# A retention layer with a two-layer network behind it: the first two groups ordered by a list scheduler, loads in one software queue, transposes moved to DMA

## The chip, the core and the metric

The kernel runs on one NeuronCore of a Trainium2 chip. Its engines take their instructions in program order, each from its own stream: TensorE (PE, with its weight loads as PEld), VectorE (DVE), ScalarE (ACT), GpSimd (POOL) and SyncE (SP). DMAs are issued from SP's stream (the hardware queue q1) or from POOL's (the software queue q0), and are moved by 16 DMA engines that all queues share. The metric is the device time of one execution in microseconds; lower is better. A profiled execution gives a span, from the first to the last instruction.

## What is computed

For 4 sequences and 8 heads of width 64, over 768 steps, a state is decayed and updated, and read by q; then two matrices with `h * cos(h)` between them act on all 3,072 tokens.

```python
for t in range(S):                       # gamma = 1 - 2**(-5 - head)
    state = gamma * state + einsum('bhd,bhe->bhde', k[:, :, t], v[:, :, t])
    y[:, :, t] = scale * einsum('bhd,bhde->bhe', q[:, :, t], state)
x = y.transpose(0, 2, 1, 3).reshape(3072, 512)
h = x @ w_in                             # 512 x 2048
out = (h * cos(h)) @ w_out               # 2048 x 512
```

## The kernel before, in words

**Tiling.** Time is cut into chunks of 128 steps, six to a sequence. Two sequences go together, so there are 12 *pairs* p (two sequences b, one chunk c = p mod 6), and two pairs make a *group* g of 512 tokens, six in all. Within a chunk the recurrence is a masked product of q and k; what came before enters through the state.

**Steps of a pair.** *Load*: q, k, v of each of the two sequences, 128 steps on the partitions, 256 KB each, in float32 (`load`, L103). *Convert* to bf16, with the decay multiplied into q and v (`conv_q` L146, `conv_v` L151, `conv_k` L156). *T* (`stage_t`, L163): 16 TensorE transposes of q and k by an identity, into PSUM, and two copies to `qkt`. *A* (`stage_a`, L182): 16 products of k and q, row-tiled, two at a time, into four PSUM banks. *Masks* (`stage_m`, L197): four on VectorE. *Y* (`stage_y`, L205): the masked A times v plus q times the old state, column-tiled, copied by ScalarE into `xt`, which is x transposed. *S* (L227): k times v added up in the bank `st_ps`, copied into `stb` for the next pair.

**Steps of a group.** *F*: for each of 16 row blocks f of w_in four matmuls of 128 x 512 into a bank (`unit_f`, L250), cosine on ScalarE (the Sin table with half pi added, L244), the product on VectorE into `gt` (L248). A half unit (`pair_f`, L258) does two f for the 256 tokens of one pair, with eight matmuls of 128 x 256. *O* (`unit_o`, L274): for each 128 tokens j sixteen matmuls of 128 x 512 with w_out, in four parts, then a copy by ScalarE and a 256 KB store from SP.

**What sets the order.** It is written out by hand; each engine's stream follows the order of the program text. Semaphore waits come from the tiles that are read and written. PSUM has seven rotating banks (`Banks`, taken and given in the order of the text) beside `st_ps`; converted tiles have three buffers, float32 loads five, `cosb` three, `ob` four. L289 to L304 issue the first loads: SP's queue gets all q and the first v of most pairs, POOL's queue k, the other v, and both weight matrices (float32 in memory, bf16 in the core), with POOL's own conversions between. L310 to L355 interleave pairs 0 to 3 with half units of groups 0 and 1. From L359 on a loop over g does, in each of 16 slots s, one F unit of group g (not for g = 1, whose F is done already) and one part of O of group g-1; eight slots go to each pair p = 2(g+1) and p+1: T at r = 1, A at 2, conversions of pair p+1 at 4, Y and S at 6, loads of pair p+3 after that.

Of the kernel before, what the change touches and what calls it, by code (L numbers as in the profile page):

```python
# [10 lines left out]
FP32 = mybir.dt.float32  # L11
# [5 lines left out]
class Banks:  # L17
# [8 lines left out]
    def give(self, t):  # L26
        self.free_list.append(t)


@with_exitstack  # L30
def kernel(
# [11 lines left out]
    C = 128  # L43
# [8 lines left out]
    PRE = 5  # L52

# [4 lines left out]

# [10 lines left out]

# [8 lines left out]


    qf = [[sb([128, H, D], FP32, f"qf{i}_{b}") for b in range(2)] for i in range(PRE)]  # L80
    kf = [[sb([128, H, D], FP32, f"kf{i}_{b}") for b in range(2)] for i in range(PRE)]
    vf = [[sb([128, H, D], FP32, f"vf{i}_{b}") for b in range(2)] for i in range(PRE)]
    ob = [sb([128, DM], FP32, f"ob{i}") for i in range(4)]
    NB = 3
# [15 lines left out]

    SRC = {"q": (qf, q), "k": (kf, k), "v": (vf, v)}

    def load(eng, p, names):  # L103
        bp, c = divmod(p, NC)
        for n in names:
            t, src = SRC[n[0]]
            b = int(n[1])
            eng.dma_start(
                out=t[p % PRE][b],
                in_=src[2 * bp + b, :, ds(c * C, C)].rearrange("h t d -> t h d"))  # L110

    def load_w_in(r):
        nc.gpsimd.dma_start(
            out=w_in_sb[:, :, ts(r, 512)],
            in_=moe_w_in[:, ts(r, 512)].rearrange("(i p) f -> p i f", p=128))
# [5 lines left out]


    nc.gpsimd.iota(pos, pattern=[[C, NC]], base=1, channel_multiplier=1,
                   allow_small_or_imprecise_dtypes=True)
    load(nc.sync, 0, ("q0", "q1", "v0"))
    load(nc.sync, 1, ("q0", "q1"))
    load(nc.gpsimd, 0, ("k0", "k1", "v1"))
    make_identity(nc, ident)
    nc.vector.memset(lnsc, math.log(scale))
    nc.vector.memset(halfpi, math.pi / 2.0)  # L130
    nc.vector.memset(mask, 1.0)
# [4 lines left out]
    nc.scalar.activation(out=gk, in_=lgp, func=AF.Exp, scale=-1.0)  # L136
    nc.gpsimd.affine_select(out=mask, in_=mask, compare_op=ALU.is_ge, fill=0.0,
# [5 lines left out]
    def bc(g, c):  # L143
        return g[:, c, :].unsqueeze(2).to_broadcast([128, H, D])

    def conv_q(p, eng):  # L146
        for b in range(2):
            eng.tensor_tensor(out=qs[p % NB][:, b], in0=qf[p % PRE][b],
                              in1=bc(gq, p % NC), op=ALU.mult)

    def conv_v(p, eng):  # L151
        for b in range(2):
            eng.tensor_tensor(out=vs[p % NB][:, b], in0=vf[p % PRE][b],
                              in1=bc(gk, p % NC), op=ALU.mult)

    def conv_k(p, on_act):  # L156
        for b in range(2):
            if on_act:
                nc.scalar.copy(out=ks[p % NB][:, b], in_=kf[p % PRE][b])
            else:  # L160
                nc.vector.tensor_copy(out=ks[p % NB][:, b], in_=kf[p % PRE][b])

    def stage_t(p, split):  # L163
        n = p % NB
        for b in range(2):
            bank = banks.take()
            tr = bank.bitcast(BF16).rearrange("p (w a t) -> p w a t", w=2, a=HP)
            for w, src in enumerate((qs[n], ks[n])):
                for a in range(HP):
                    nc.tensor.transpose(tr[:, w, a, :], src[:, b, 2 * a : 2 * a + 2, :], ident)  # L170
            if split and b == 1:
                nc.vector.tensor_copy(out=qkt[n][:, b], in_=tr)
            else:
                nc.scalar.copy(out=qkt[n][:, b], in_=tr)
            banks.give(bank)

    def qt(n, b, a):
        return qkt[n][:, b, 0, a, :]

    def kt(n, b, a):  # L180
        return qkt[n][:, b, 1, a, :]
    def stage_a(p):  # L182
        n = p % NB
        todo = []
        for b in range(2):
            bk = [banks.take(), banks.take()]
            ap = [t.rearrange("p (a t) -> p a t", a=HP) for t in bk]
            for a in range(HP):
                for j in range(2):
                    po = 64 * j  # L190
                    nc.tensor.matmul(ap[j][:, a, :], lhsT=kt(n, b, a)[po : po + 64, :],
                                     rhs=qt(n, b, a)[po : po + 64, :],
                                     tile_position=(po, 0))
            todo.append((b, bk, ap))
        return todo

    def stage_m(p, item):  # L197
        b, bk, ap = item
        for j in range(2):
            nc.vector.tensor_tensor(  # L200
                out=am[p % 2][b][j], in0=ap[j],
                in1=mask.unsqueeze(1).to_broadcast([128, HP, 128]), op=ALU.mult)
            banks.give(bk[j])

    def stage_y(p, copy_st=nc.vector.tensor_copy):  # L205
        c = p % NC
        n = p % NB
        for b in range(2):
            bank = banks.take()
            yp = bank.rearrange("p (a t) -> p a t", a=HP)  # L210
            for a in range(HP):
                if c > 0:
                    for j in range(2):
                        nc.tensor.matmul(  # L214
                            yp[ts(j, 64), a, :], lhsT=stb[p % 2][:, b, a, ts(j, 64)],
                            rhs=qt(n, b, a), start=True, stop=False,
                            skip_group_check=True)
                for j in range(2):
                    nc.tensor.matmul(
                        yp[ts(j, 64), a, :], lhsT=vs[n][:, b, 2 * a + j, :],  # L220
                        rhs=am[p % 2][b][j][:, a, :], start=(c == 0), stop=True,
                        skip_group_check=True)
            nc.scalar.copy(out=xt[(p // 2) % 2][:, :, ts(2 * (p % 2) + b, C)], in_=yp)
            banks.give(bank)
        if c == NC - 1:
            return
        for b in range(2):  # L227
            for a in range(HP):
                for j in range(2):
                    h = 2 * a + j  # L230
                    nc.tensor.matmul(  # L231
                        st_ps[ts(j, 64), b, a, :], lhsT=ks[n][:, b, h, :],
                        rhs=vs[n][:, b, h, :], start=(c == 0 and b == 0 and a == 0),
                        stop=True, skip_group_check=True)
        for j in range(2):
            copy_st(out=stb[(p + 1) % 2][ts(j, 64), :, :, ts(j, 64)], in_=st_ps[ts(j, 64)])  # L236


    f_no = [0]

    def act(bank, out):
        cb = cosb[f_no[0] % 3]
        f_no[0] += 1
        nc.scalar.activation(out=cb, in_=bank, func=AF.Sin, bias=halfpi)  # L244
        if len(out.shape) == 3:
            cb = cb.rearrange("p (f t) -> p f t", f=2)
            bank = bank.rearrange("p (f t) -> p f t", f=2)
        nc.vector.tensor_tensor(out=out, in0=bank, in1=cb, op=ALU.mult)  # L248

    def unit_f(g, f):  # L250
        bank = banks.take()
        for i in range(KIN):
            nc.tensor.matmul(bank, lhsT=w_in_sb[:, i, ts(f, 128)], rhs=xt[g % 2][:, i, :],  # L253
                             start=(i == 0), stop=(i == KIN - 1))
        act(bank, gt[g % 2][:, f, :])
        banks.give(bank)

    def pair_f(p, r):  # L258

        g, hf = divmod(p, 2)  # L260
        for f in (4 * r, 4 * r + 2):
            bank = banks.take()
            for e in range(2):
                for i in range(KIN):
                    nc.tensor.matmul(bank[:, ts(e, 256)], lhsT=w_in_sb[:, i, ts(f + e, 128)],  # L265
                                     rhs=xt[g % 2][:, i, ts(hf, 256)],
                                     start=(i == 0 and e == 0), stop=(i == KIN - 1),
                                     skip_group_check=True)
            act(bank, gt[g % 2][:, f : f + 2, ts(hf, 256)])
            banks.give(bank)  # L270

    o_bank = {}

    def unit_o(g, j, part):  # L274
        if part == 0:
            o_bank[0] = banks.take()
        bank = o_bank[0]
        for f in range(4 * part, 4 * part + 4):
            nc.tensor.matmul(bank, lhsT=gt[g % 2][:, f, ts(j, 128)], rhs=w_out_sb[:, f, :],  # L279
                             start=(f == 0), stop=(f == KOUT - 1))  # L280
        if part == 3:
            o = ob[j % 4]
            nc.scalar.copy(out=o, in_=bank)
            banks.give(bank)
            bp, c = divmod(2 * g + j // 2, NC)
            nc.sync.dma_start(out=out[ds((2 * bp + j % 2) * S + c * C, C), :], in_=o)


    load(nc.gpsimd, 1, ("k0", "k1", "v0", "v1"))  # L289
    load_w_in(0)  # L290
    load_w_in(1)
    for p in (2, 3):
        load(nc.sync, p, ("q0", "q1"))
# [8 lines left out]
    for r in range(4):  # L302
        load_w_out(r)
# [109 lines left out]
```

## Time and profile before

| | |
|---|---|
| runs of the kernel | 225.5 us median of 3 (224.25 to 225.9) |
| profiled execution | 223.9 us span; the page gives no other total for it |
| PE, DVE, ACT, POOL busy | 207.6, 124.4, 121.2, 83.4 us |
| granted TensorE clock | 1.000 |
| first matmul; first F of group 2; last matmul | 4.89; 78.67; 219.9 us |
| DMA | 29.65 MB written (27.26 MB read from memory): queue q1 37,776 packets for 14.95 MB, q0 7,344 for 14.42 MB |

The profile is read by stretches, since the share of busy time hides where it is lost: the 40 slices of the page show which engine is full when. The chain that ended last is followed back from the last instruction, and gives for each piece its start, its length and what it was. Columns of a stretch are its bounds, then per engine the busy time and the instructions, the granted clock, the DMA engines' share and GB/s written. A matmul of 512 columns is shown with 379 ns, but they overlap: four of them follow one another in 0.864 us.

### The profile page before, as it was taken

What the parts mean: (1) busy time and instruction counts of PE and PEld (TensorE: products, weight loads), DVE (VectorE), ACT (ScalarE), POOL (GpSimd) and SP (SyncE); (2) the same over time, 40 slices, a digit from 0 to 9 for tenths busy, and PEclk for the clock granted to TensorE, in tenths of its full rate; (3) what the DMA queues carried; (4) which work ended last, traced back from release to release, by engine and by line L of the source; (5) the groups of instructions that cost most, each with busy time, mean ns of one, the idle gap of its engine ahead of it and who ended that gap; (6) DMA issues with size and microseconds to landing.
All of it is one profiled execution on the core that took longest, in us unless ns stands there. A gap on an engine that the chain in (4) does not pass through costs nothing.

```text
span 223.9 us, 4434 instructions
## 1 busy us (share of the span) xinstructions
PE 207.6 (93%) x1792; PEld 118.7 (53%) x1792; DVE 124.4 (56%) x201; ACT 121.2 (54%) x180; POOL 83.4 (37%) x95
## 2 busy tenths in 40 slices
PE   1479899989999999999999999999999999999992
PEld 0357788958655554554554554554554544444440
DVE  4375969979583727638538528528527333443000
ACT  3475897766625255565565565565565545444121
POOL 7989848603999957190520610000000000000000
PEclk9999999999999999999999999999999999999999
DMA  6999999999949793925511511011011011110221
GB/s 159 333 233 274 220 282 199 197 298 259 276 97 314 216 268 76 256 81 171 129 47 59 132 47 53 0 50 47 0 50 47 0 50 47 47 47 0 97 78 63
DMA packets 45140, 29.65 MB, mean 132 GB/s; under 512 B 35456, under 2 KB 39552, under 8 KB 45120
## 3 DMA queue, kind: packets, MB, share of 16 engines
q1 hardware_dynamic: 37776, 14.95, 26.1%
q0 software_dynamic: 7344, 14.42, 25.4%
q8 instruction: 14, 0.23, 0.4%
q14 instruction: 6, 0.05, 0.1%
HBM read 27.26 MB, written 6.29 MB: 150 GB/s over the span
## 4 chain that ended last, share of the span: by engine, by line
PE 83%; DMA 4%; ACT 4%; DVE 4%; SPq 2%; issue 1%; DVEq 0%; ACTq 0%
PE bank_64 L279 15%; PE bank_63 L279 6%; PE bank_67 L253 5%; PE bank_69 L253 5%; PE bank_65 L253 5%; PE bank_66 L279 5%; DMA qf_1_81<-in_q_dram 4%; PE bank_68 L279 4%; PE bank_66 L253 4%; PE bank_68 L253 4%; PE bank_63 L253 4%; PE bank_65 L279 3%; PE bank_63 L265 2%; PE bank_69 L265 2%; PE bank_66 L265 2%; PE bank_68 L265 2%
## 5 line engine op out<-in xcount | busy, mean ns | idle before, releaser
L253 PEld LDWEIGHTS <-w_in_sb 128*128 128x128 bf16 x256 | 23.8, 98 | 26.9
L279 PEld LDWEIGHTS <-gt_137 128*128 128x128 bf16 x192 | 18.8, 98 | 22.7
L279 PEld LDWEIGHTS <-gt_136 128*128 128x128 bf16 x192 | 18.3, 98 | 21.4
L265 PEld LDWEIGHTS <-w_in_sb 128*128 128x128 bf16 x256 | 25.2, 100 | 5.1 <-issue 0.8
L279 PE MATMUL bank_64<-w_out_sb,gt_136 128*128 128x512 bf16 x96 | 24.2, 380 | 0.0
L279 PE MATMUL bank_64<-w_out_sb,gt_137 128*128 128x512 bf16 x64 | 16.4, 379 | 0.0
L279 PE MATMUL bank_63<-w_out_sb,gt_136 128*128 128x512 bf16 x48 | 12.3, 379 | 0.0
L279 PE MATMUL bank_66<-w_out_sb,gt_137 128*128 128x512 bf16 x48 | 11.8, 379 | 0.0
L236 DVE CAST stb_133<-st_ps 64x512 bf16<-64x512 f32 x10 | 6.9, 687 | 2.6 <-PE st_ps L231 2.4
L253 PE MATMUL bank_63<-xt_134,w_in_sb 128*128 128x512 bf16 x32 | 8.2, 380 | 0.0
L279 PE MATMUL bank_68<-w_out_sb,gt_137 128*128 128x512 bf16 x32 | 8.2, 379 | 0.0
L279 PE MATMUL bank_65<-w_out_sb,gt_136 128*128 128x512 bf16 x32 | 7.9, 380 | 0.0
L244 ACT ACTIVATE cosb_140<-bank_65,halfpi 128x512 bf16<-128x512 f32 x8 | 5.5, 689 | 4.3 <-PE bank_65 L253 3.3
L244 ACT ACTIVATE cosb_139<-bank_67,halfpi 128x512 bf16<-128x512 f32 x7 | 4.8, 687 | 5.3 <-PE bank_67 L253 4.3
L244 ACT ACTIVATE cosb_138<-bank_69,halfpi 128x512 bf16<-128x512 f32 x7 | 4.9, 693 | 4.6 <-PE bank_69 L253 4.3
L214 PEld LDWEIGHTS <-stb_133 128*64 128x64 bf16 x96 | 5.2, 109 | 3.8 <-issue 3.8
L253 PE MATMUL bank_68<-xt_135,w_in_sb 128*128 128x512 bf16 x28 | 7.2, 379 | 0.0
L244 ACT ACTIVATE cosb_138<-bank_63,halfpi 128x512 bf16<-128x512 f32 x7 | 4.8, 689 | 3.6 <-PE bank_63 L253 2.2
L244 ACT ACTIVATE cosb_140<-bank_67,halfpi 128x512 bf16<-128x512 f32 x6 | 4.1, 691 | 4.5 <-PE bank_67 L253 4.3
L244 ACT ACTIVATE cosb_138<-bank_66,halfpi 128x512 bf16<-128x512 f32 x6 | 4.1, 687 | 4.1 <-PE bank_66 L253 2.4
L253 PE MATMUL bank_65<-xt_134,w_in_sb 128*128 128x512 bf16 x24 | 6.2, 380 | 0.0
L253 PE MATMUL bank_67<-xt_134,w_in_sb 128*128 128x512 bf16 x24 | 6.2, 380 | 0.0
(398 smaller groups left out, 518.5 us busy)
## 6 DMA issues: line engine op xcount, KB each, us to landing
w_in_sb<-in_moe_w_in_dram POOLq DMA_DIRECT2D x4, 512.0 KB, 10.2
w_out_sb<-in_moe_w_out_dram POOLq DMA_DIRECT2D x4, 512.0 KB, 15.4
out_dram<-ob_108 SPq DMA_DIRECT2D x6, 256.0 KB, 2.1
out_dram<-ob_109 SPq DMA_DIRECT2D x6, 256.0 KB, 2.0
out_dram<-ob_110 SPq DMA_DIRECT2D x6, 256.0 KB, 2.1
out_dram<-ob_111 SPq DMA_DIRECT2D x6, 256.0 KB, 2.0
qf_0_78<-in_q_dram SPq DMA_DIRECT2D x3, 256.0 KB, 4.4
qf_1_79<-in_q_dram SPq DMA_DIRECT2D x3, 256.0 KB, 5.0
```

Source lines behind the costliest of these rows:

```text
L214: nc.tensor.matmul(yp[ts(j, 64), a, :], lhsT=stb[p % 2][:, b, a, ts(j, 64)], rhs=qt(n, b, a), start=True, stop=False, skip_group_check=True)
L236: copy_st(out=stb[(p + 1) % 2][ts(j, 64), :, :, ts(j, 64)], in_=st_ps[ts(j, 64)])
L244: nc.scalar.activation(out=cb, in_=bank, func=AF.Sin, bias=halfpi)
L253: nc.tensor.matmul(bank, lhsT=w_in_sb[:, i, ts(f, 128)], rhs=xt[g % 2][:, i, :], start=(i == 0), stop=(i == KIN - 1))
L265: nc.tensor.matmul(bank[:, ts(e, 256)], lhsT=w_in_sb[:, i, ts(f + e, 128)], rhs=xt[g % 2][:, i, ts(hf, 256)], start=(i == 0 and e == 0), s ...
L279: nc.tensor.matmul(bank, lhsT=gt[g % 2][:, f, ts(j, 128)], rhs=w_out_sb[:, f, :], start=(f == 0), stop=(f == KOUT - 1))
```

## The change

Pairs 0 to 5, A of pair 6, F of groups 0 and 1 and O of group 0 are no longer ordered by hand: while the program is built, a list scheduler (`Plan`) places each step on an engine, by ranks, its own costs, free banks and supposed landing times of loads, and emits the steps in the order of their starts. Group 0's first four f are half units, the other twelve whole units over both pairs; group 1 stays in half units. All loads but q of pair 0 go through POOL, both sequences in one DMA of 512 KB, in the order of `LOADS`; the scheduler puts VectorE, ScalarE or GpSimd on conversions and copies. Pairs 5 to 11 (the sixth pair on, `DMA_T`) have q and k transposed by two DMAs each from SP, between tiles in the core, in place of T. The loop starts at g = 2; loads of pair p+3, conversions and transposes of pair p+1 are issued at r = 0 of pair p, and after slot r = 3 one block does A of pair p+1, then Y and S of pair p, then the masks. The last O tile is done in two halves of 256 columns, stored from SP and ACT. The Sin table is loaded at the start, and the identity is made by a VectorE fill and one GpSimd step.

```diff
+class Plan:
...
+    def run(self, start, cold_until=0.0):
+        free = dict(start)
+        mode = [None]
+        left = list(self.ops)
+        t = 0.0
+        while left:
...
+                best = None
+                for op in left:
+                    if e not in op["engines"]:
+                        continue
+                    r = self.ready(op)
+                    if r is None:
+                        continue
+                    if r > t + 1e-9:
+                        nxt.append(r)
+                        continue
+                    ok = True
+                    for k, n in op["take"]:
+                        tk = sorted(self.tokens[k])
+                        n += op["spare"] if k == "bank" else 0
+                        if len(tk) < n:
+                            ok = False
+                        elif tk[n - 1] > t + 1e-9:
+                            nxt.append(tk[n - 1])
...
+                    key = (op["rank"] + (0.5 if op["mode"] and op["mode"] != mode[0] else 0), op["n"])
+                    if best is None or key < best[0]:
+                        best = (key, op)
+                if best is None:
+                    continue
+                op = best[1]
+                left.remove(op)
+                c = op["cost"][e] if isinstance(op["cost"], dict) else op["cost"]
+                busy, took = c if isinstance(c, tuple) else (c, c)
+                if e == "E":
...
+                        busy, took = busy + self.SWITCH, took + self.SWITCH
+                        mode[0] = op["mode"]
+                for k, n in op["take"]:
+                    self.tokens[k].sort()
+                    del self.tokens[k][:n]
+                op.update(eng=e, start=t, free=t + busy, done=t + took, lat=self.LAT[e])
+                free[e] = t + busy
+                if op["mb"]:
+                    self.dma = max(self.dma, t + busy + 1.6) + op["mb"] / op["rate"]
...
+    def emit(self):
+        for op in sorted(self.ops, key=lambda o: (o["start"], o["n"])):
+            op["fn"](op["eng"])
...
-    def load(eng, p, names):
-        bp, c = divmod(p, NC)
-        for n in names:
-            t, src = SRC[n[0]]
-            b = int(n[1])
-            eng.dma_start(
-                out=t[p % PRE][b],
-                in_=src[2 * bp + b, :, ds(c * C, C)].rearrange("h t d -> t h d"))
+    def load(eng, p, names):
+        bp, c = divmod(p, NC)
+        for n in names.split():
+            t, src = SRC[n[0]]
+            if len(n) == 1:
+                eng.dma_start(
+                    out=t[p % PRE].rearrange("p b h d -> p (b h) d"),
+                    in_=src[ds(2 * bp, 2), :, ds(c * C, C), :].rearrange(
+                        "b h t d -> t (b h) d"))
...
+    def dma_t(p, w):
+        n = p % NB
+        nc.sync.dma_start_transpose(
+            out=qkt[n][:, w].rearrange("p b a t -> p (b a) t"),
+            in_=(qs, ks)[w][n].rearrange("p b h d -> p (b h d)"))
...
     nc.scalar.activation(out=gq, in_=lgp, func=AF.Exp, bias=lnsc)
     nc.scalar.activation(out=gk, in_=lgp, func=AF.Exp, scale=-1.0)
+    nc.scalar.activation(out=lnsc, in_=halfpi, func=AF.Sin)
+    nc.gpsimd.affine_select(out=ident, in_=ident, compare_op=ALU.not_equal, fill=1.0,
+                            base=0, pattern=[[-1, 128]], channel_multiplier=1)
+    load(nc.gpsimd, 0, "v")
...
-    def stage_t(p, split):
-        n = p % NB
-        for b in range(2):
-            bank = banks.take()
-            tr = bank.bitcast(BF16).rearrange("p (w a t) -> p w a t", w=2, a=HP)
-            for w, src in enumerate((qs[n], ks[n])):
-                for a in range(HP):
-                    nc.tensor.transpose(tr[:, w, a, :], src[:, b, 2 * a : 2 * a + 2, :], ident)
...
-    load(nc.gpsimd, 1, ("k0", "k1", "v0", "v1"))
-    load_w_in(0)
-    load_w_in(1)
-    for p in (2, 3):
-        load(nc.sync, p, ("q0", "q1"))
-    load(nc.sync, 4, ("q0", "q1", "v0"))
-    conv_v(0, nc.gpsimd)
-    conv_v(1, nc.gpsimd)
-    load(nc.gpsimd, 2, ("k0", "k1", "v0", "v1"))
-    load_w_in(2)
-    load_w_in(3)
-    load(nc.gpsimd, 3, ("k0", "k1", "v0", "v1"))
-    conv_v(2, nc.gpsimd)
-    for r in range(4):
-        load_w_out(r)
-    load(nc.gpsimd, 4, ("k0", "k1", "v1"))
...
-    conv_q(0, nc.vector)
-    conv_k(0, True)
-    stage_t(0, True)
-    m0 = stage_a(0)
-    masks(0, m0)
-    conv_k(1, True)
-    conv_q(1, nc.vector)
-    stage_y(0, nc.scalar.copy)
-    stage_t(1, True)
-    pair_f(0, 0)
-    m1 = stage_a(1)
-    masks(1, m1)
-    pair_f(0, 1)
-    stage_y(1, nc.scalar.copy)
-    conv_q(2, nc.vector)
-    conv_k(2, True)
-    pair_f(1, 0)
-    pair_f(1, 1)
-    stage_t(2, False)
-    pair_f(0, 2)
-    m2 = stage_a(2)
...
-    for r in range(4):
-        pair_f(3, r)
...
+    at = lambda tm: dict(start=0.0, free=0.0, done=tm, lat=0.0)
+    ld["q", 0, 0], ld["q", 0, 1], ld["k", 0, 0], ld["k", 0, 1] = map(at, (3.9, 4.8, 5.9, 6.7))
+    ld["v", 0, 0] = ld["v", 0, 1] = at(8.3)
+    LOADS = ["q1", "k1", "v1", "w0a", "w0b", "w1", "w2", "w3", "q2", "k2", "v2", "q3", "k3", "v3",
+             "o0", "o1", "o2", "o3", "q4", "k4", "v4", "q5", "k5", "v5", "q6", "k6", "v6",
+             "q7", "k7", "v7", "q8", "k8", "v8"]
+    conv_op = {}
+    pend = []
+    for i, x in enumerate(LOADS):
+        if x[0] in "qkv":
+            p = int(x[1:])
+            o = add("P", 1.2, lambda e, p=p, n=x[0]: load(nc.gpsimd, p, n),
+                    [("issued", prev)] if prev else [], 50 + i, [("sem", 1)], [("sem", 1)],
...
+    for p in range(PL + 1):
+        c = p % NC
+        for b in range(2):
+            T["cq", p, b] = add("D" if p < 2 else "DP" if p < 3 else "P", TT, lambda e, p=p, b=b: conv_q(p, b, e),
+                                [ld["q", p, b], G("tq", p - NB, b), G("dt", p - NB, 0)],
+                                10 * p + b, name="cq%d%d" % (p, b))
...
+        if p < DMA_T:
+            for b in range(2):
+                for w, x in enumerate("qk"):
+                    T["t" + x, p, b] = add(
+                        "E", 0.225, lambda e, p=p, b=b, w=w: t_mm(p, b, w),
+                        [T["c" + x, p, b]] + ([T["tq", p, b]] if w else []), 10 * p + 1,
...
+                        [T["t" + x, p, b], T.get(("eq", p, b)) if w else None] + old,
+                        10 * p + 0.5, (), [("bank", 1)] if w else [], name="e%s%d%d" % (x, p, b))
+            kq = {b: [T["eq", p, b], T["ek", p, b]] for b in range(2)}
+        else:
+            for w, x in enumerate("qk"):
+                T["dt", p, w] = add("S", (1.3, 4.6), lambda e, p=p, w=w: dma_t(p, w),
+                                    [T["c" + x, p, 0], T["c" + x, p, 1]] + old, 10 * p,
+                                    name="dt%d%d" % (p, w))
+            kq = {b: [T["dt", p, 0], T["dt", p, 1]] for b in range(2)}
+        for b in range(2):
+            T["a", p, b] = add("E", 0.225, lambda e, p=p, b=b: a_mm(p, b), kq[b], 10 * p + 2,
...
+                                [T["y", p, b]] + done, 10 * p + 5, (), [("bank", 1)],
+                                name="yc%d%d" % (p, b))
+        units = []
+        if p in (2, 3):
+            units = [("h", p, f) for f in range(0, 16, 2)]
+        elif p == 0:
...
+    plan.run({"S": 2.5, "P": 5.2, "A": 4.2, "D": 3.6, "E": 1.0}, COLD)
+    plan.emit()
...
+    def block(p):
+        nxt = p + 1 < NP
+        if nxt:
+            a_mm(p + 1, 0)
+            a_mm(p + 1, 1)
+        for b in range(2):
+            y_mm(p, b)
+            y_copy(p, b, "A")
+        if p % NC < NC - 1:
+            s_mm(p)
+            for j in range(2):
+                s_copy(p, j, "D")
+        if nxt:
+            for b in range(2):
+                for j in range(2):
+                    a_mask(p + 1, b, j)
+    def conv(p):
+        for b in range(2):
+            conv_k(p, b, "D")
+        for b in range(2):
+            conv_q(p, b, "P")
+        for b in range(2):
+            conv_v(p, b, "P")
+        for w in range(2):
+            dma_t(p, w)
...
-    for g in range(1, NG + 1):
-        for s in range(16):
-            hf, r = divmod(s, 8)
-            p = 2 * (g + 1) + hf
-            if 1 < g < NG:
-                unit_f(g, s)
-            unit_o(g - 1, *divmod(s, 4))
-            if p < NP:
-                if r == 1:
-                    stage_t(p, False)
-                elif r == 2:
-                    todo = stage_a(p)
-                    stage_m(p, todo[0])
-                elif r == 3:
-                    stage_m(p, todo[1])
-                elif r == 4 and p + 1 < NP:
-                    conv_q(p + 1, nc.gpsimd)
-                    conv_k(p + 1, False)
-                    conv_v(p + 1, nc.gpsimd)
-                elif r == 6:
-                    stage_y(p)
-                    if p + 3 < NP:
-                        load(nc.sync, p + 3, ("q0", "q1", "v0"))
-                        load(nc.gpsimd, p + 3, ("k0", "k1", "v1"))
+    for g in range(2, NG + 1):
+        for s in range(16):
+            hf, r = divmod(s, 8)
+            p = 2 * (g + 1) + hf
+            if p < NP and r == 0:
+                if p + 3 < NP:
+                    load(nc.gpsimd, p + 3, "q k v")
+                if p + 1 < NP:
+                    conv(p + 1)
+            if g < NG:
+                f_mm(g, s)
+                f_cos(("f", g, s))
+                f_mul(g, s)
+            if g == NG and s == 12:
+                last_o(NG - 1, 3)
+                break
+            o_mm(g - 1, *divmod(s, 4))
+            if s % 4 == 3:
+                o_out(g - 1, s // 4, "A")
+            if p < NP and r == 3:
+                block(p)
...
+    def last_o(g, j):
+        o = ob[o_no[0] % 4]
+        for hf in range(2):
+            bank = banks.take()
+            for f in range(KOUT):
+                nc.tensor.matmul(bank[:, :256], lhsT=gt[g % 2][:, f, ts(j, 128)],
+                                 rhs=w_out_sb[:, f, ts(hf, 256)],
+                                 start=(f == 0), stop=(f == KOUT - 1))
+            copy("AD"[hf], o[:, ts(hf, 256)], bank[:, :256])
+            (nc.sync, nc.scalar)[hf].dma_start(
+                out=out[ds(o_row(g, j), C), ts(hf, 256)], in_=o[:, ts(hf, 256)])
...
```

## The prediction, made before the changed kernel was run

> **What bounds the kernel now.** I read the page's first two parts, then the chain that ended last, first its beginning, then one turn of the steady loop, then busy time and bandwidth in chosen stretches, then the single groups.
>
> ```profile
> span 223.9 us, 4434 instructions
> PE 207.6 (93%) x1792; PEld 118.7 (53%) x1792; DVE 124.4 (56%) x201; ACT 121.2 (54%) x180; POOL 83.4 (37%) x95
> PE   1479899989999999999999999999999999999992
> DMA  6999999999949793925511511011011011110221
> ```
>
> TensorE is the bound from the sixth slice on. What isn't matmul lies in the first 25 us, while the DMA engines are full for some 60 us. The beginning of the chain:
>
> ```profile
> 4.51 10.03 DMA qf_1_81<-in_q_dram
> 14.56 1.20 DVE qs_113 L148
> 15.81 1.03 PE bank_65 L170 x8
> 16.85 1.85 PE bank_66 L265 x8
> ...
> 25.24 1.03 PE bank_69 L265 x8
> 26.27 0.87 PE bank_63 L265 x8
> ```
>
> Pair 1's second q tile, issued by SP at 4.51, lands only at 14.56. Eight 256-column matmuls take 1.85 us at 16.85 and 0.87 later: the array is at half rate until about 20. One turn of the steady loop (L170 transposes, L191 A, L231 S, L253 and L279 the big products), from the same chain:
>
> ```profile
> 82.13 0.45 PE bank_65 L170 x8
> 82.58 0.45 PE bank_69 L170 x8
> 83.02 0.86 PE bank_63 L253 x4
> ...
> 85.30 0.97 PE bank_69 L253 x4
> 86.27 0.86 PE bank_68 L279 x4
> ...
> 109.62 0.25 PE st_ps L231 x16
> 109.87 0.97 PE bank_68 L253 x4
> ```
>
> A pair's transposes cost 0.90 us of TensorE. The product after A or S takes 0.97 in place of 0.86, so a return from row- or column-tiled matmuls costs about 0.11. There is no idle time here: what leaves TensorE shortens the span. Busy time by stretch; the last two columns are DMA share and GB/s written:
>
> ```profile
> 36.00:44.00 8.00, 8.00 (x118) 7.33 (x115) 7.94 (x14) 6.06 (x10) 6.37 (x7) 1.00 1.22 197
> 46.00:50.00 4.00, 3.24 (x43) 2.33 (x43) 3.95 (x7) 2.56 (x5) 0.00 (x0) 1.00 1.11 326
> 52.00:56.00 4.00, 4.00 (x39) 3.59 (x37) 3.94 (x8) 3.02 (x5) 1.95 (x2) 1.00 1.04 237
> ```
>
> Weights (written as bf16, half of what is read) move at 197, so some 360 to 390 read; q/k/v in both queues at 326; SP's queue alone at 237, equally full. SP's queue is the slow one.
>
> **What the skill says.** "TensorE: Matmul & The Clock Gate", Part 1: the array runs at half rate until a window of about 3.4 us was busy. The 1.85 against 0.87 agrees. "DMA: Bandwidth & Descriptors", section Latency and other measured facts: DMA transposes reach 261 GB/s; its section Anatomy of one DMA gives each DMA 2.0 us fixed. The trace has no transpose; its 256 KB stores land in 2.1. "SBUF — State Buffer", Who interferes with whom: a VectorE cast in the two-port mode and GpSimd shut each other out of a shared port. The trace agrees; the same cast, beside GpSimd's work and alone:
>
> ```profile
> L161 DVE CAST ks_117<-kf_1_89 x1: 1920/1920/1920, 65.0 to 65.0; 128x512 bf16<-128x512 f32 x1
> L161 DVE CAST ks_116<-kf_1_97 x1: 421/421/421, 53.8 to 53.8; 128x512 bf16<-128x512 f32 x1
> ```
>
> **The change, part by part**, against the span of 223.9. The runs' median is 225.5, 1.6 more (their lowest 0.35 more); I carry the difference over.
>
> *Loads.* SP keeps two issues, q of pair 0; the rest goes through POOL, 512 KB at a time. POOL takes 0.88 us for 256 KB (1,024 rows of 256 bytes) and 0.75 for weights (512 longer rows), so about 1.15 for 2,048 rows by that slope: 460 GB/s, above the transfer rate, so issuing hides behind it; without that cover, some 0.3 us per load. Pair 1's q is now complete after 2.1 MB. The two-microsecond stretches carry 229, 280, 322 and 333 GB/s from 2 to 10 us, so 2.1 MB have landed at about 9.3, against 14.56; k at 10.8, v at 12.3. For bounds later on: 3.15 MB by 12.3; w_in's 4.2 at 360 to 390, 24; 1.57 a pair at 345, pair 3 at 33; w_out, 44 to 45; pair 6 at 58.
>
> *The first two pairs.* What is late next is VectorE. Until pair 1's last mask it has 8 conversions, 8 masks and one product, each 0.60 in pitch, and four half copies at about 0.33: 11.5 us. From pair 0's A on (about 9.0, against 9.75, as k0's second half has no v or second q load beside it) 4 masks, a conversion of v, four conversions of pair 1, three copies, 4 masks and a product remain: 14 x 0.60 + 1.0 = 9.4, with some 1.5 of waits on a still cold TensorE: last mask at 20, S done at 21. Before, it ended at 24.8. If the array is warm at 15, 20; if only at 20, 22. The early load of the Sin table (1.28) lies in ScalarE's 4.0 us wait for k0, and costs 1.3 if k0 were early; the other identity costs nothing, as the first transpose waits for q0's conversion (3.93 + 0.69) anyway.
>
> *From there to group 2's first F.* Before: 25.24 to 78.67, 53.4 us. Its content: 28 halves or units at 0.87 (24.4), O of group 0 (16 x 0.865 = 13.8), pairs 2 to 5 with T 0.90, A 0.66 with its return, Y and S 1.38 (pair 5 1.13): 11.5 in all; 49.7, so 3.7 idle. Changed: two more units (+1.74), T of pair 5 off (-0.90), A of pair 6 in (+0.55): 51.1. The listed order changes the array's tiling 40 times before the loop where the old one does 23 times; 15 of them lie in this part, 15 x 0.10 = 1.5. Old waits here were copies of T and masks queued behind other work, 0.4 to 1.9 each, which a list by readiness can fill; I keep 1.5 for loads that come later than listed. 21 + 51.1 + 1.5 + 1.5 = 75.1: **-3.6**.
>
> *The loop.* Before: 78.67 to the last matmul at 219.9, 141.2 = 144 products x 0.864 (124.4) + six T (5.4) + six A (4.0) + Y and S (7.4). Changed: no T, five A (pair 6's is in the part before), and A's return falls in five blocks: 5.4 + 0.66 + 5 x 0.11 = **-6.6**. The bank order leaves room: the second Y takes the bank of the last F, done 0.86 + 0.55 + 0.45 = 1.86 earlier, and cosine and product need 0.69 + 0.69 + 0.25.
>
> *The added wait.* A of pair p+1 waits for two DMA transposes. From the slot where they are issued to the block there are four F and four O, 6.9 us. SP first finishes the previous store (copy 0.58, issue 0.33): q's transpose is issued at 1.2. k's follows both casts on VectorE (two at 0.42 behind a product, 1.9; up to 4.9 if GpSimd holds the port at 1.9 each) and q's own issue. An issue has no row: between a store's 0.33 and the 2.3 of a crowded SP load; I take 1.4, so k's starts at 2.6. Its flight: 262 KB at 261 GB/s is 1.0, plus 2.0 fixed, plus its issue: 4.4 as an estimate from the page, landing at 7.0. high end 10, three times the transfer part and a second issue. A late k holds A, and behind it on TensorE everything; stores on SP wait behind a waiting transpose, but ob's four buffers cover those. Estimate 0.2 x 5 = **+1.0**. A gain from this wait is excluded; its gain is T, counted above.
>
> *The tail.* The last O tile in two column halves: 32 x 256 columns cost what 16 x 512 did; the last copy is half of 0.58, the last store half of 256 KB: **-0.3**.
>
> Sum: -3.6 - 6.6 + 1.0 - 0.3 = -9.5; span 214.4, median **216**.
>
> **The rivals.** *Better than that (0.12):* no load is late, transposes hidden, the array warm early: -5.9 - 6.6 - 0.4, 212.6. For it: the copies that cost the old waits had free engines beside them. *Loads late (0.14):* the TensorE order is fixed beforehand; if the one queue reads 310 rather than 345 to 390, pair 4 lands 4 to 6 us later, with pairs 4 and 5 waited for: 220 to 221. For it: no stretch shows the software queue alone; against: its packets are long (7,344 for 14.4 MB, against 37,776 for 15.0). *Slower: transposes late (0.16):* landing after slot + 6.9, in five blocks; every microsecond more costs five. From k's flight of 4.4 on that is 5 x; 9.5 are used up at 6.3. With 8 us: +18, 234, and more at pairs 5 and 6 before the loop. For it: no row prices the operation. Against: the DMA engines are nearly idle by then (shares 0.1 to 0.5). *The change does less than it says:* only the order of the first part could fail to hold, and that is the load case.
>
> **How the numbers follow.** Forecast 0.58 (213.5 to 219), better 0.12, loads late 0.14 (0.11 of it faster, 0.03 same), transposes late 0.16 (0.14 slower, 0.02 same). Faster by over 1%, about what a measurement can tell here: 0.81; within: 0.05; slower: 0.14. The range 211.5 to 224 leaves out most of the transpose case and a thin lower edge.
>
> **What would show it.** In the changed profile: pair 1's q conversion at 9 to 13; S of pair 1 done near 21; the first L343 product of group 2 near 75; no L265 transposes after that; five blocks with A, Y and S in one piece of about 1.9 us and waits of A on a DMA transpose under 0.5 us each. Waits of several microseconds there, or gaps on TensorE between 30 and 65 ended by a load, would make it wrong.

## The result, and the profile after

The changed kernel takes 237.0 us (median of 4 runs, 236.3 to 238.2) against 225.7: 1.053 times the kernel before, with an interval of 1.048 to 1.057. It is slower, where the forecast was 216. Of the runs behind the numbers below, five that came out more than 1.5% above the fastest of their kernel are left out, four of them in the first experiment. The profiled execution of the changed kernel has a span of 234.5 us against 223.9. From the first two parts of its page:

```profile
span 234.5 us, 4107 instructions
PE 203.4 (87%) x1648; PEld 110.4 (47%) x1648; DVE 122.1 (52%) x204; ACT 110.6 (47%) x177; POOL 89.0 (38%) x91
PE   1577999979869990099999999999999999999993
PEclk9999999999999998559999999999999999999999
DMA  7999999999999999900810816408201111101212
```

TensorE has 4 us less busy time than before, and two slices (of 5.9 us each) in which it does nothing; in the two slices after 94 us its clock is at half. The chain of work that ended last, around this place (its columns are start, length, what):

```profile
73.72 7.77 PE bank L388 x36
81.49 0.86 PE bank L343 x4
82.35 0.86 PE bank L388 x4
83.22 0.86 PE bank L343 x4
84.08 0.71 PE bank L388 x4
84.79 15.34 DMA qkt<-ks
100.13 0.05 issue
100.17 1.03 PE bank L288 x13
101.21 1.00 PE bank L312 x16
102.20 0.43 PE st_ps L329 x16
102.63 1.82 PE bank L343 x4
104.45 1.71 PE bank L388 x4
106.16 0.97 PE bank L343 x4
```

The first block of the loop waits for the transpose of pair 7's k, which takes 15.34 us from issue to landing. TensorE stands still for 11.8 of them, from 88.4 on. Then A, Y, S and two products run at half rate: 1.03 for 0.55, 1.82 for 0.97 and so on, 2.9 us together. "TensorE: Matmul & The Clock Gate" of the Trainium skill (Part 1) says that the clock falls to half after an idle window of about 3.4 us and is released after a busy one of the same length. Here the array stood for 11.8 us, and the half rate lasted 6.0 us of work, from 100.2 to 106.2, longer than one such window. Busy time by stretch of four microseconds at that place (last columns: clock, DMA share, GB/s):

```profile
84.00:88.00 4.00, 4.00 (x20) 1.78 (x19) 1.38 (x2) 1.80 (x3) 3.98 (x5) 1.00 1.48 349
88.00:92.00 4.00, 0.40 (x2) 0.00 (x0) 0.69 (x1) 0.84 (x2) 0.92 (x1) 1.00 0.97 36
92.00:96.00 4.00, 0.00 (x0) 0.00 (x0) 0.00 (x0) 0.00 (x0) 0.00 (x0) 0.57 1.14 183
96.00:100.00 4.00, 0.00 (x0) 0.00 (x0) 0.00 (x0) 0.00 (x0) 0.00 (x0) 0.50 1.09 324
100.00:104.00 4.00, 3.83 (x52) 2.71 (x53) 1.30 (x2) 1.07 (x2) 1.50 (x2) 0.50 0.05 19
```

The DMA engines are full all the while, first with loads and stores at 349 GB/s, then with almost nothing that counts in bytes, then with loads again. What they load is seen in GpSimd's stream:

```profile
75.63 1.45 POOL L210 DMA_DIRECT2D qf<-in_q_dram  x1
77.08 1.15 POOL L210 DMA_DIRECT2D kf<-in_k_dram  x1
78.22 1.15 POOL L210 DMA_DIRECT2D vf<-in_v_dram  x1
...
83.37 1.19 POOL L210 DMA_DIRECT2D qf<-in_q_dram  x1
84.56 1.15 POOL L210 DMA_DIRECT2D kf<-in_k_dram  x1
85.70 1.15 POOL L210 DMA_DIRECT2D vf<-in_v_dram  x1
```

These are the loads of pairs 10 and 11, the last of the kernel. In the program's text they stand in the turns of pairs 7 and 8, but nothing holds GpSimd back until then: it had free buffers and issued the loads of four pairs, 8 to 11, between 64.8 and 86.9 us.

By stretches, changed against before: the part up to the first F of group 2 ends at 81.3 instead of 78.5 (+2.8); from there to the end of the last matmul 149.6 instead of 141.3 (+8.2 before rounding, of which 11.8 + 2.9 are the wait and the half rate, so -6.5 without them); the tail 3.6 instead of 4.05 (-0.4). The sum is +10.6, the difference of the spans.

### The profile page after: what moved, and what is told of

Its sections match the earlier page's. It is cut to its first block, busy times and chain, and to the rows that moved or that the text cites. A ratio compares the mean times of both kernels' runs of the same rounds, so it can differ in the third digit from the quotient of the medians.

```text
span 234.5 us, 4107 instructions
## 1 busy us (share of the span) xinstructions
PE 203.4 (87%) x1648; PEld 110.4 (47%) x1648; DVE 122.1 (52%) x204; ACT 110.6 (47%) x177; POOL 89.0 (38%) x91
## 4 chain that ended last, share of the span: by engine, by line
PE 71%; DMA 16%; POOL 5%; ACT 2%; DVE 2%; issue 1%; SPq 0%; POOLq 0%; DVEq 0%; ACTq 0%
PE bank L388 32%; PE bank L343 26%; DMA qkt<-ks 7%; DMA qf<-in_q_dram 6%; PE bank L364 3%; DMA qkt<-qs 3%; PE bank L288 2%; PE bank L307 2%; PE bank L312 2%; POOL w_in_sb L221 2%; PE bank L405 1%; ACT cosb L351 1%; PE st_ps L329 1%; DVE ks L236 1%; POOL vf L210 1%
## 5 line engine op out<-in xcount | busy, mean ns | idle before, releaser
L351 ACT ACTIVATE cosb<-bank,halfpi 128x512 bf16<-128x512 f32 x96 | 65.6, 687 | 72.9 <-PE bank L343 60.1
L388 PE MATMUL bank<-w_out_sb,gt 128*128 128x512 bf16 x368 | 91.6, 382 | 0.0
L355 DVE TENSOR_TENSOR gt<-bank,cosb 128x512 bf16<-128x512 f32 x76 | 51.9, 689 | 57.7 <-ACT cosb L351 57.4
L343 PE MATMUL bank<-xt,w_in_sb 128*128 128x512 bf16 x304 | 78.1, 383 | 0.0
L388 PEld LDWEIGHTS <-gt 128*128 128x128 bf16 x368 | 35.9, 98 | 43.3 <-issue 1.1
L246 POOL TENSOR_TENSOR vs<-vf,gk 128x512 bf16<-128x512 f32 x20 | 20.7, 1054 | 39.0 <-issue 25.3
L294 DVE TENSOR_TENSOR am<-bank,mask 128x512 bf16<-128x512 f32 x48 | 30.0, 682 | 2.0 <-PE bank L288 1.7
L234 ACT COPY ob<-bank 128x512 f32<-128x512 f32 (+1 forms) x24 | 13.9, 577 | 21.9 <-PE bank L388 20.7
L234 ACT CAST xt<-bank 128x512 bf16<-128x512 f32 x24 | 13.4, 588 | 20.1 <-PE bank L312 20.0
L288 PE MATMUL bank<-qkt 64*128 64x128 bf16 x192 | 9.0, 232 | 14.7 <-DMA qkt<-ks 11.8
L364 PE MATMUL bank<-xt,w_in_sb 128*128 128x256 bf16 x160 | 19.9, 278 | 0.4 <-ACT xt L234 0.4
L242 POOL TENSOR_TENSOR qs<-qf,gq 128x512 bf16<-128x512 f32 x19 | 19.9, 1070 | 0.7 <-DMA qf<-in_q_dram 0.6
L372 DVE TENSOR_TENSOR gt<-bank,cosb 128x512 bf16<-128x512 f32 x20 | 13.4, 684 | 7.9 <-ACT cosb L351 7.8
## 6 DMA issues: line engine op xcount, KB each, us to landing
kf<-in_k_dram POOLq DMA_DIRECT2D x11, 512.0 KB, 10.6
```

The lines of the kernel that those rows point to most:

```text
L234: nc.scalar.copy(out=out, in_=in_)
L242: ENG[e].tensor_tensor(out=qs[p % NB][:, b], in0=qf[p % PRE][:, b], in1=bc(gq, p % NC), op=ALU.mult)
L246: ENG[e].tensor_tensor(out=vs[p % NB][:, b], in0=vf[p % PRE][:, b], in1=bc(gk, p % NC), op=ALU.mult)
L294: nc.vector.tensor_tensor(out=am[p % 2][b][j], in0=bank.rearrange("p (a t) -> p a t", a=HP), in1=mask.unsqueeze(1).to_broadcast([128, HP, ...
L355: nc.vector.tensor_tensor(out=gt[g % 2][:, f, :], in0=bank, in1=cb, op=ALU.mult)
```

## The experiments

All times are medians in us, with the ratio to the kernel before in the same series.

**The loads one pair later.** Theory *collision*: the transposes are late because the software queue moves loads beside them. Rival: what stands ahead of them in SP's queue.

```diff
-                if p + 3 < NP:
-                    load(nc.gpsimd, p + 3, "q k v")
                 if p + 1 < NP:
                     conv(p + 1)
+                if p > 6 and p + 2 < NP:
+                    load(nc.gpsimd, p + 2, "q k v")
```

> The loads of pairs 9 to 11 are issued by POOL one pair later and behind the conversions, so that they no longer fill the DMA engines while pair 7's transposes are in flight. Theory 'collision' (pair 7's transposes landed 15.3 us after their issue because the software queue moved loads beside them): the wait of 11.8 us at 88.4 and the half rate after it, some 3 us, are gone; span 219 to 221, run 221 to 223. Rival 'order in SP's queue' (they were late because stores stood ahead of them, or because their first use in the loop is late): a wait of at least 8 us stays, run 233 or more.

Measured: 226.6, ratio 1.0026 (1.0002 to 1.0050), span 224.9. Some 10 of the expected 15 us are back. The chain shows why:

```profile
85.06 7.50 DMA qkt<-ks
92.56 0.05 issue
92.61 0.62 PE bank L288 x16
...
103.74 4.76 DMA qkt<-ks
108.50 0.05 issue
108.54 0.62 PE bank L288 x16
```

GpSimd issues the moved loads from 80.0 and 96.1 on, and the next transposes are issued at 83.4 and 102.1, while the loads still move. I had moved each burst onto another transpose, one pair's loads at a time. The transposes that TensorE waits for now take 7.5 and 4.8 us where one took 15.3, and it stands still for 3.4 and 0.5 us in these two turns, which is 3.9 of the 5 us that are missing. The size of the expectation was missed; the rival, which asked for 233 or more, falls.

**Pair 7 on TensorE**, all loads where they are.

```diff
-        for w in range(2):
-            dma_t(p, w)
+        if not (p == 7):
+            for w in range(2):
+                dma_t(p, w)
...
+            if p + 1 < NP and r == 1 and (lambda p: p == 7)(p + 1):
+                for b in range(2):
+                    for w in range(2):
+                        t_mm(p + 1, b, w)
+                    for w in range(2):
+                        t_copy(p + 1, b, w, "AD"[w])
```

> Pair 7 alone is transposed by TensorE (16 transposes and four copies in slot 1), all loads stay where they are. Collision: nothing waits for a transpose while the loads run, minus 15, plus about 1 for the TensorE transposes; run 222 to 225. Rival 'the burst of loads itself is what is late' (then something else of that time, a conversion or a load, waits in its place): 229 or more.

Measured: 222.25, ratio 0.984 (0.978 to 0.989). One pair's two DMA transposes decide between 5% slower and 1.6% faster. Time from issue to landing of its twelve transposes:

```profile
DMA to landing us min/median/max: 2.7/2.7/6.9
```

In the changed kernel this line has 2.7, 4.7 and 15.3.

**Loads put beside the transposes**, in the kernel with pair 7 on TensorE, which had none there: GpSimd waits for the k conversion of pairs 9, 10 and 11 and then loads an earlier pair's q, k, v into their own buffers once more. Nobody waits for these loads.

```diff
+        if p in (9, 10, 11):
+            nc.gpsimd.tensor_copy(out=gate, in_=ks[p % NB][:, 1, 7, 62:64])
+            load(nc.gpsimd, p - 2, "q k v")
```

> On top of the run with pair 7 on TensorE: three 512 KB loads that nobody waits for go into the software queue just as the transposes of pairs 9, 10 and 11 are issued (POOL waits for the k conversion, then loads q, k, v of an earlier pair into their own buffers again). Collision: each of these transposes lands 4 to 11 us later and A waits in three turns, 3 to 8 us each; run 231 to 246. Rival (it was the stores ahead in SP's queue or the first turn): no wait, 222 to 223.

Measured: 232.6, ratio 1.034 (1.027 to 1.041), some 10 us more than without them; the profiled executions are 12.7 apart in span (233.2 and 220.5). The chain's pieces of DMA in the three turns, and busy time by stretch in the first:

```profile
115.92 7.18 DMA qkt<-ks
136.04 6.40 DMA qkt<-ks
155.44 7.53 DMA qkt<-ks
```

```profile
120.00:122.00 2.00, 0.34 (x2) 0.00 (x0) 0.69 (x1) 0.79 (x2) 2.00 (x3) 1.00 1.31 129
122.00:124.00 2.00, 0.85 (x16) 0.75 (x16) 0.00 (x0) 0.00 (x0) 0.90 (x1) 0.80 1.10 297
124.00:126.00 2.00, 2.00 (x44) 1.91 (x42) 0.00 (x0) 0.59 (x1) 0.00 (x0) 0.50 1.04 356
126.00:128.00 2.00, 2.00 (x26) 1.02 (x20) 1.46 (x3) 0.97 (x2) 0.00 (x0) 0.84 0.11 39
```

Transposes of 2.7 us become 6.4 to 7.5 in every turn that has loads beside it. Of the 12.7, TensorE's waits at A are 8.0 us together; most of the rest is the half rate that follows, in the first turn clock 0.50 to 0.84 from 124 to 128. With this and the run before, the collision is shown: loads beside a transpose that is needed four slots later make the wait, and without the loads or without the transpose it is not there.

**No DMA transpose at all**: TensorE transposes all 12 pairs, in the listed part and in slot 1 of the loop.

```diff
-    DMA_T = 5
+    DMA_T = 99
...
```

> All 12 pairs are transposed by TensorE, in the listed part too. Against the changed kernel: the wait and the half rate off (-15), the waits for pair 6's transposes off (-2), seven times T at 0.9 plus copies on VectorE and ScalarE (+6.3 to 7). Collision: 226 to 228, about the time of the kernel before, since the listed part of the changed kernel is slower than the old one by 3 and the loop's block saves 1. If the DMA transposes hurt in a way beyond the one collision (a slower loop), below 224.

Measured: 226.7, ratio 1.0042 (1.0022 to 1.0061). What remains of the change, the listed part, the single queue, the block and the halved tail, brings nothing together: the first F of group 2 starts at 81.9 in its profile, against 78.5 before (+3.4), and the loop and the tail give back 2.6 of that.

**Only the transposes**, in the kernel before.

```diff
...
                 if r == 1:
-                    stage_t(p, False)
+                    if p < 6:
+                        stage_t(p, False)
...
                     conv_k(p + 1, False)
+                    if p + 1 > 5:
+                        for w in range(2):
+                            nc.sync.dma_start_transpose(
+                                out=qkt[(p + 1) % NB][:, w].rearrange("p b a t -> p (b a) t"),
+                                in_=(qs, ks)[w][(p + 1) % NB].rearrange("p b h d -> p (b h d)"))
```

> The kernel before, with its order by hand and its two load queues, and only the transposes of pairs 6 to 11 moved to DMAs from SP, issued with the conversions, six slots (10.4 us) ahead of A. If transposes are hidden where no burst of loads stands beside them: minus 6 x 0.9, run 219.5 to 221. If two queues of loads beside them make them late as in the changed kernel: A waits in some of the six turns, run 226 or more.

Measured: 220.6, ratio 0.978 (0.972 to 0.984): six times T, 5.4 us, is gained to within 0.3. Here the transposes stand six slots ahead of A, and no A waits for one, although loads of both queues still run at that time (DMA shares of 0.52 to 1.17 by stretches of 4 us from 76 to 104). The collision has not gone: from issue to landing the twelve transposes take 2.7 us in the median and up to 6.8, but they stand six slots ahead, 10.4 us of TensorE's work.

**What makes the listed part long.** In the profile with pair 7 on TensorE the chain of that part holds a VectorE cast of k of 2.76 us and, right behind it, the transposes of pair 6 (6.95 from issue to landing, A waits 2.0). Two runs take one each away. First, pairs 5 and 6 are transposed by TensorE too:

```diff
-    DMA_T = 5
+    DMA_T = 7
```

> On top of the run with pair 7 on TensorE: pairs 5 and 6 too are transposed by TensorE, so no DMA transpose runs before pair 8. The wait of 1.9 to 2.0 us of pair 6's A and the one of ScalarE and VectorE work ahead of it (0.9) go, two T at 0.9 and eight copies come. Collision in the listed part: 221 to 222.5, a draw. If the transposes cost more there than their two waits (through SP and what stands behind them): below 221.

Measured: 222.8, ratio 0.988 (0.985 to 0.991); a draw against 222.25, as expected. Then the k conversions of the listed part are left to ScalarE:

```diff
-            T["ck", p, b] = add("DA", SB2, lambda e, p=p, b=b: conv_k(p, b, e),
+            T["ck", p, b] = add("A", SB2, lambda e, p=p, b=b: conv_k(p, b, e),
```

> On top of the run with pair 7 on TensorE: the scheduler may put conversions of k in the listed part on ScalarE only, so VectorE's casts no longer meet GpSimd's conversions there (2.28 and 2.76 us in place of 0.42 in the profiles). Theory 'shared port': the listed part ends 1.5 to 3 us earlier, run 219.5 to 221. Rival 'ScalarE is as full there': 222 or more.

Measured: 219.9, ratio 0.974 (0.970 to 0.978); the first F of group 2 starts at 79.4 instead of 81.6. In the four profiles whose listed part is that of the changed kernel it starts between 81.3 and 82.2, so the step is clear of their spread. VectorE's casts of k with pair 7 on TensorE:

```profile
L236 DVE CAST ks<-kf x12: 417/420/2827, 49.3 to 146.0; 128x512 bf16<-128x512 f32 x12
```

and with the k conversions of the listed part on ScalarE:

```profile
L236 DVE CAST ks<-kf x10: 415/418/1258, 74.0 to 143.8; 128x512 bf16<-128x512 f32 x10
```

The scheduler books a cast at one fixed price, 0.42 us, but beside GpSimd's conversions it takes up to seven times as long. Keeping these casts off VectorE in the listed part gains 2.4; the list is made anew for this run, so what else moved in it is in the 2.4 as well.

**The hand order with the good parts**: the kernel before, with DMA transposes, conversions at r = 0, A(p+1), Y(p), S(p) in one block at r = 6, and the last O in halves.

```diff
+            if p >= 6 and r == 0 and p + 1 < NP:
+                convs(p + 1)
...
+            if r == 6:
+                if p >= 6 and p + 1 < NP:
+                    todo = stage_a(p + 1)
+                stage_y(p)
+                if p >= 6 and p + 1 < NP:
+                    stage_m(p + 1, todo[0])
+                    stage_m(p + 1, todo[1])
+                loads(p + 3)
```

> The hand order and both load queues of the kernel before, with DMA transposes from pair 6 on, conversions two slots after the last Y, A of the next pair in one block with Y and S from pair 6 on, and the last O tile in halves. If the listed part and the single queue bring nothing by themselves: run with DMA transposes alone (220.6) minus 0.11 for each of five blocks minus 0.45 at the tail, 219.5 to 220. If the listed part was worth its work, this cannot come below the 222.3 of the listed kernel without the collision by more than 1.

Measured: 219.9, ratio 0.975 (0.970 to 0.979). In span it is 0.8 under the run with the transposes alone, near the expected 1.0; in the runs the difference is within their spread. It is 2.4 below the listed kernel without the collision (222.25), more than the 1 that the expectation allowed if the listed part was worth its work; and it draws with the listed kernel whose casts are on ScalarE (219.9). Last, the second copy of T goes to VectorE for pairs 4 and 5:

```diff
-                stage_t(p, False)
+                stage_t(p, True)
```

> On top of the hand order with the block: for pairs 4 and 5 the second copy of the transposes goes to VectorE (as it does for pairs 0 and 1), so that A does not wait for two ScalarE copies of 1.0 us in a row (1.94 and 1.03 us of the chain). Minus 1 to 2: run 218 to 219. If VectorE is late there instead: no change, 220.

Measured: 218.9 (6 runs), ratio 0.969 (0.967 to 0.971). This version beats both kernels, by 3.1% and 7.6%, without the scheduler and with both load queues.

## Why the prediction was wrong

The steps that held: T, A's return and the block in the loop, forecast at -6.6, are -6.5 when the wait and the half rate are taken off; the run with pair 7 on TensorE agrees, its loop is 135.7 us, 5.6 shorter than before, with one T of 0.9 put back. The tail, forecast at -0.3, is -0.4. The issue of a 512 KB load, estimated at 1.15 us, takes 1.15. Span and forecast are 20.1 us apart: 13.7 of it is the added wait (14.7 where +1.0 stood), 6.4 the listed part (+2.8 where -3.6 stood).

**The step that failed** is "The added wait", with the sentence that it rested on in the rivals: "the DMA engines are nearly idle by then (shares 0.1 to 0.5)". That was a misreading of the profile before, in the first place. The DMA row of its page, which the prediction shows, has 9, 3 and 9 in the three slices from 78 to 95 us, and by stretches of 4 us:

```profile
80.00:84.00 4.00, 4.00 (x32) 2.32 (x31) 1.38 (x2) 2.34 (x4) 1.70 (x3) 1.00 0.88 271
88.00:92.00 4.00, 4.00 (x20) 1.76 (x18) 2.87 (x6) 1.89 (x3) 0.36 (x1) 1.00 0.94 264
```

Only from 112 us on are the shares between 0 and 0.6. In the second place, these shares are those of the kernel before, where GpSimd and SP issue the late loads in the turns in which they stand, since half of each pair (q and half of v) goes through SP's queue, behind its waits, and the last of it is issued at 122.6 us. I had counted what the loads cost to issue and when they land for their own users, but not that the single queue, held up by no such waits, would empty the rest of the program into the DMA engines by 87 us, on top of the first transposes of the loop. The estimate of the flight without company was even too high: 4.4 worked out from "DMA: Bandwidth & Descriptors" against 2.7 measured. (The 2.0 us fixed in it is what that page's section on one DMA states for the software queue; the transposes go through the hardware queue.) In company the flight was 15.3; my high end had the transpose of k landing 10 us after its slot begins, which leaves it a flight of some 7.4.

**The rival was the right one, its arithmetic not.** "Transposes late" had 0.16. I priced it as five turns at 5 us for each microsecond; it was one turn with 11.8, and four with none, plus 2.9 of half rate that I had not counted at all. That the 237.0 measured lies near the rival's 234 is chance.

**The listed part**, forecast at -3.6, is +2.8. S of pair 1 is done at 22.4, not at 21: the early loads run at 244, 287, 233 and 231 GB/s in the four stretches from 2 to 10 us where I took 229, 280, 322 and 333, which the two queues together had shown, so v of pair 0 is awaited until 9.77 and k of pair 1 until 13.1. From there to 81.3 TensorE is idle for 5.6 by the trace, where I had kept 1.5. A run shows 2.2 of it, the casts beside GpSimd; I had quoted that very pair of rows, 1,920 against 421 ns, and used it for the loop, where it did no harm, but not for the listed part, where VectorE and GpSimd convert at once. By the waits in the trace, 1.9 is the wait for pair 6's transposes, which collide with the loads of pairs 7 to 9; transposing by TensorE instead costs as much as it gains. The two amounts are not independent, since those transposes are issued behind the casts. The rest is read from the waits and was not tried: 0.9 for a cast of k, 0.8 for a cosine, 0.7 for GpSimd's q and 0.4 each for three copies on ScalarE.

**What stays open.** Why a transpose becomes so slow beside loads was not settled. A transpose is 1,024 packets of 256 bytes, 18 ns each when alone. If engines took turns packet by packet with the loads' 4 KB packets (195 ns), two transposes, 128 packets per engine, would be held up by the 24 packets per engine of a pair's loads, some 4.7 us, and that is about what the run with loads beside shows. But from 89 to 94 us in the changed kernel nearly all packets in the trace are the transposes', many of them at 200 to 400 ns each, with load packets only as fast as one engine moves them (two or three in half a microsecond); the bulk of the loads that GpSimd had issued by 86.9 doesn't move until 94. So turns of packets alone don't explain this stretch. Nor was it tried whether loads from a hardware queue alone do the same harm.

## What to carry to other kernels

A queue that was made faster empties as soon as buffers are free: before a DMA is put on a critical path, ask what is *issued* by then on the queue that has just lost its brake, not only what the old profile shows in that place, and read the old profile there in short stretches. Place such a DMA far ahead of its use (six slots instead of four left no wait here), or tie the bulk loads to something that keeps them away from it; one pair later was another transpose. A scheduler with fixed prices is blind to engines that hold each other up (a cast booked at 0.42 us took up to 2.83); and a long wait on TensorE is paid twice, once in waiting and once in clock.

## What the hardware showed that I had not expected

A DMA transpose of 128 x 1024 bf16 between tiles in the core lands 2.7 us after its issue, where I had estimated 4.4, and holds SP for 1.3; beside software-queue loads it took 4.8 to 15.3, and an issue up to 4.75. A wait of 2.8 us was enough to bring the array to half rate for the next 3 (from 123.2 on in the run with loads beside, clock 0.50 from 124 to 126), while one of 3.4 in the run with later loads left it at full rate. So the length of the wait alone did not decide it; what else does was not tried.
